# The end of a fused attention and spectral-mix kernel: late rows of Z copied in place, two tiles per store, products begun earlier

## The chip, the cores and the metric

The kernel runs on one core of a Trainium2 chip. The metric is the device time of one execution in microseconds. Three timed runs of the kernel before gave 465.42, 465.90 and 469.37 us, a median of 465.9.

## The reference

A causal attention with a window of 128 positions and a linear bias by head gives x, and a spectral layer mixes x over the sequence:

```python
# q, k, v: (8 batches, 8 heads, 576 positions, 64);  w_r, w_i: (64 modes, 512, 512);  w_ch: (512, 512)
scores = q @ k.T / sqrt(64) - slope[h] * |i - j|     # only 0 <= i - j < 128
x = softmax(scores) @ v                              # as (8, 576, 512)
X = rfft(x, axis=1)[:, :64]                          # Xr + i Xi
Yr = einsum('bmd,mde->bme', Xr, w_r) - einsum('bmd,mde->bme', Xi, w_i)
Yi = einsum('bmd,mde->bme', Xr, w_i) + einsum('bmd,mde->bme', Xi, w_r)
y = irfft(Yr + 1j * Yi, n=576, axis=1)
u = x + y
out = u + relu(u @ w_ch)
```

All inputs and the output are float32. The two sets of mode weights are 134 MB together and are read once.

## The kernel before

The inverse transform is a product with a fixed matrix, FT (128 rows: 64 modes, real and imaginary), so y = FT.T Z, where Z holds a batch's 128 rows of Yr and Yi. Then u @ w_ch = x @ w_ch + FT.T (Z @ w_ch), with Z @ w_ch called ZW. The parts that need only x can be done while the mode weights still come in.

**Stages.** The attention runs over 32 units (8 batches, 4 pairs of heads). The weights of the first head pair's 128 channels are worked off beside it, 3 modes at a time. Then comes the stream: the other 384 channels, one mode per step, for 64 modes. `_load_w` (L578) issues two loads a mode on SP's queue, `wr` and `wi`, into a ring of three buffers. `_modes` does 24 products a mode (L613, L617) into the PSUM tile `acc`, and after each eighth mode and after modes 60, 62 and 64 DVE adds the result to the first pair's part and writes it to `ZT` (L632), which is Z transposed.

The order of each engine's instructions is the order in which the program issues them (a manual schedule). Within the stream, after the products of each mode, the kernel before adds other work:

- **x @ w_ch** for the 36 tiles of 128 positions (`g.seq`: each batch has four tiles; two batches share a ninth with their last 64 positions each). `_xt` transposes the tile (four products into `tp`, a DVE copy to `xT`). `_xw` multiplies it with w_ch into the PSUM tile `xw` (L659, L661), four products of 512 columns, and a fifth that adds x itself where the tile goes by way q. Then `xw` is split into two bf16 parts, `hl`: for each half of the partitions an ACT copy (L666) and a DVE subtraction of that copy (L667). The 36 tiles are spread evenly over the stream.
- **FT** (`_ft`, four times): five transposes and four reorderings, each with four POOL copies into a shared tile `order`, two products and two ACT copies.
- **The early rows of Z and ZW** (`_z_early`, one batch per mode at modes 51 to 58): 16 products of 512 columns into `zwp` and 16 of 128 columns into `zp`, in turn, copied to `ZZ` by ACT and DVE (L688, L689). They give the rows of the modes up to 48 in their final places. The last 16 modes' 32 rows sit in a place that depends on the batch (`_block`).

**PSUM.** In the stream: one bank for `acc`, two buffers each for `tp` and `xw`, one each for `zp` and `zwp`. In the end: three pairs `mm`, `y` (pool `fps`) and two banks for the late rows.

**The end** (`_finish`). After the last mode `_z_late` does the late rows of batches 0 to 3: 16 products for ZW (L700) and 16 for Z (L706) into `late`. Batch 0's are copied to `ZZ` by ACT and DVE (L710, L711); an ACT copy (L713) writes all to `zl`, and three DMAs (L716) carry the other batches' rows to their partitions. The same is done for batches 4 to 7 after tile 4, with four DMAs. Then each tile i goes through:

- `_known`: `hl` into `mm`, and x into `y` (way a only); pairs of products of 512 columns, each for 64 positions (L648). Tiles 0 to 2 have this before the last mode.
- FT.T ZW into `mm`, FT.T Z into `y`, a pair each.
- way a: ACT relu of `mm` to `r` (L766), DVE `y` + `r` (L775). Way q: ACT copies `y` (L769), DVE takes max(`mm`, x) (L770), POOL adds (L778). 19 tiles go by q, 17 by a.
- the store, one DMA of 256 KB a tile (L747), or two of 128 KB for the shared tiles (L749), on SP's queue, from six output buffers.

Of the kernel before, what the change touches and what calls it, by code (L numbers as in the profile page):

```python
# [25 lines left out]
TAIL = 2  # L26

# [6 lines left out]
def kernel(  # L34
# [52 lines left out]
    g.way = ["q" if 2 <= i < len(g.seq) - 3 and i % 5 in (0, 2, 4) else "a" for i in range(len(g.seq))]  # L87

    with tc.manual_schedule(engines={ET.SP, ET.PE, ET.Activation, ET.DVE, ET.Pool}):
        with ExitStack() as wctx:  # L90
# [88 lines left out]
            g.ZZ = zp.tile([P, B, 2, DM], BF16)  # L179
            last = len(GROUPS) - 1  # L180
            for t in line[ahead:]:
                _load_w(g, *t)
            with ExitStack() as xctx:
                xt = xctx.enter_context(tc.tile_pool(name="xts", bufs=2))
                xps = xctx.enter_context(
                    tc.tile_pool(name="xps", bufs=2, space=bass.MemoryType.PSUM))
                eps = xctx.enter_context(
                    tc.tile_pool(name="eps", bufs=1, space=bass.MemoryType.PSUM))
                todo, done, k = list(tiles[last]), 0, 0
                xT = _xt(g, 0, xt, xps)  # L190
                while done < NM - 4:
                    m0, mg = todo.pop(0)
                    _modes(g, last, m0, mg, last=True)
                    done = m0 + mg

                    while k < len(g.seq) and k * (NM - 6) < done * len(g.seq):
                        nxt = _xt(g, k + 1, xt, xps) if k + 1 < len(g.seq) else None
                        _xw(g, k, xT, xps)
                        xT, k = nxt, k + 1
                    if done % 8 == 4 and done < 36:  # L200
                        _ft(g, done // 8, xt, xps)
                    for b in range(B):
                        if m0 <= NM - 14 + b < done:
                            _z_early(g, b, eps)
            g.fps = ctx.enter_context(
                tc.tile_pool(name="fps", bufs=3, space=bass.MemoryType.PSUM))
            g.mm, g.y = {}, {}
            for m0, mg in todo[:-1]:
                _modes(g, last, m0, mg, last=True)
            for i in range(3):  # L210
                _known(g, i)
            _modes(g, last, *todo[-1], last=True)
# [89 lines left out]
def _ft(g, c, pool, psum):  # L302


    nc = g.nc
    S = g.S
    if c == 0:
        cvec = pool.tile([P, 1], FP32, tag="cvec", name="cvec", bufs=1)
        nc.vector.memset(cvec, 2.0 / S)
        nc.vector.memset(cvec[0:1], 1.0 / S)  # L310
        nc.vector.memset(cvec[64:65], 1.0 / S)
        g.FTn = pool.tile([P, S], BF16, tag="FTn", name="FTn", bufs=1)
        for st in range(g.ST):
            n = min(P, S - st * P)
            tp = psum.tile([P, 4, P], BF16, tag="tp", name="tft")[:, 0]
            nc.tensor.transpose(tp[:, 0:n], g.F[0:n, st], g.ident_b[0:n, 0:n])
            nc.vector.tensor_scalar_mul(g.FTn[:, st * P : st * P + n], tp[:, 0:n], cvec)
    order = pool.tile([P, P], BF16, tag="order", name="order", bufs=1)
    src = g.ident_b.rearrange("p (r g m) -> p g r m", r=2, g=4)
    for k in range(4):  # L320
        nc.gpsimd.tensor_copy(  # L321
            order[:, 32 * k : 32 * k + 32].rearrange("p (r m) -> p r m", r=2), src[:, _block(c, k)])
    for a, z in ((0, 512), (512, S)):
        ps = psum.tile([P, g.DM], FP32, tag="xw", name="ftp")
        nc.tensor.matmul(  # L325
            ps[:, 0 : z - a], lhsT=order, rhs=g.FTn[:, a:z], start=True, stop=True)
        nc.scalar.copy(g.FT[:, c, a:z], ps[:, 0 : z - a])
# [324 lines left out]
def _xw(g, n, xT, psum):  # L652
# [4 lines left out]
    xw = psum.tile([P, g.DM], FP32, tag="xw", name="xw")  # L657
# [13 lines left out]
def _z_early(g, b, psum):  # L671


    nc = g.nc
    zp = psum.tile([P, 4, P], FP32, tag="zp", name="zp")
    zwp = psum.tile([P, g.DM], FP32, tag="zwp", name="zwp")
    for et in range(4):
        for k in range(4):
            blk = _block(b % 4, k) % 3
            l = g.ZT[:, et, blk].rearrange("p a m b -> p (a m) b")[:, :, b]  # L680
            ks = slice(32 * k, 32 * k + 32)
            nc.tensor.matmul(
                zwp[ks], lhsT=l, rhs=g.wch[:, et], start=(et == 0), stop=(et == 3),
                tile_position=(0, 32 * k))
            nc.tensor.matmul(
                zp[ks, et], lhsT=l, rhs=g.ident_b, start=True, stop=True,
                tile_position=(0, 32 * k))
    nc.vector.tensor_copy(g.ZZ[:, b, 0], zp.rearrange("p a b -> p (a b)"))  # L688
    nc.scalar.copy(g.ZZ[:, b, 1], zwp)  # L689


def _z_late(g, b0, psum, pool, own):


    nc = g.nc
    late = psum.tile([P, 2, g.DM], FP32, tag="late", name="late")
    for et in range(4):
        for c in range(4):
            l = g.ZT[:, et, 3].rearrange("p a m b -> p (a m) b")[:, :, b0 + c]
            nc.tensor.matmul(  # L700
                late[32 * c : 32 * c + 32, 1], lhsT=l, rhs=g.wch[:, et],
                start=(et == 0), stop=(et == 3), tile_position=(0, 32 * c))
    for et in range(4):
        for c in range(4):
            l = g.ZT[:, et, 3].rearrange("p a m b -> p (a m) b")[:, :, b0 + c]
            nc.tensor.matmul(  # L706
                late[32 * c : 32 * c + 32, 0, et * P : et * P + P], lhsT=l, rhs=g.ident_b,
                start=True, stop=True, tile_position=(0, 32 * c))
    if own:
        nc.scalar.copy(g.ZZ[0:32, b0, 1], late[0:32, 1])  # L710
        nc.vector.tensor_copy(g.ZZ[0:32, b0, 0], late[0:32, 0])  # L711
    zl = pool.tile([P, 2, g.DM], BF16, tag="zl", bufs=1, name="zl")
    nc.scalar.copy(zl, late)  # L713
    for c in range(1 if own else 0, 4):
        ks = slice(32 * c, 32 * c + 32)
        nc.sync.dma_start(out=g.ZZ[ks, b0 + c], in_=zl[ks])  # L716


def _known(g, i):
# [3 lines left out]
    g.mm[i] = g.fps.tile([P, g.DM], FP32, tag="mm", name="mm")  # L723
    g.y[i] = g.fps.tile([P, g.DM], FP32, tag="y", name="y")
    _pair(nc, g.mm[i], [g.ident2] * 2, [g.hl[:, i, h] for h in range(2)], start=True, stop=False)
    if g.way[i] == "a":
        _pair(nc, g.y[i], [g.ident_b[:, 0:64], g.ident_b[:, 64:128]], [x] * 2,
              start=True, stop=False)


def _finish(g):
# [5 lines left out]
    with ExitStack() as fctx:  # L737
        pool = fctx.enter_context(tc.tile_pool(name="fin", bufs=4))
        lps = fctx.enter_context(
            tc.tile_pool(name="lps", bufs=1, space=bass.MemoryType.PSUM, side="right"))  # L740
        _z_late(g, 0, lps, pool, True)
        o, r, y = {}, {}, {}

        def store(i):
            for h, (b, s) in enumerate(g.seq[i][1]):
                if h == 0 and g.seq[i][1][1] == (b, s + 64):
                    nc.sync.dma_start(out=g.out[b, s : s + P, :], in_=o[i])  # L747
                    break
                nc.sync.dma_start(out=g.out[b, s : s + 64, :], in_=o[i][64 * h : 64 * h + 64])  # L749

        for i in range(N + 3):
            if i < N:
                if i >= 3:
                    _known(g, i)
                ft = [g.FT[:, b % 4, s : s + 64] for b, s in g.seq[i][1]]
                _pair(nc, g.mm[i], ft, [g.ZZ[:, b, 1] for b, _ in g.seq[i][1]],
                      start=False, stop=True)
                _pair(nc, g.y[i], ft, [g.ZZ[:, b, 0] for b, _ in g.seq[i][1]],
                      start=(g.way[i] == "q"), stop=True)
            if i == 4:  # L760
                _z_late(g, 4, lps, pool, False)
            j = i - 1
            if 0 <= j < N:
                r[j] = pool.tile([P, g.DM], FP32, tag="r", name="r")
                if g.way[j] == "a":
                    nc.scalar.activation(r[j], g.mm[j], AF.Relu)  # L766
                else:
                    y[j] = pool.tile([P, g.DM], FP32, tag="y", name="ys")
                    nc.scalar.copy(y[j], g.y[j])  # L769
                    nc.vector.tensor_tensor(out=r[j], in0=g.mm[j], in1=g.seq[j][0], op=ALU.max)  # L770
            j = i - 2
            if 0 <= j < N:
                o[j] = pool.tile([P, g.DM], FP32, tag="o", bufs=6, name="o")
                if g.way[j] == "a":
                    nc.vector.tensor_tensor(out=o[j], in0=g.y[j], in1=r[j], op=ALU.add)  # L775
                    store(j)
                else:
                    nc.gpsimd.tensor_tensor(out=o[j], in0=r[j], in1=y[j], op=ALU.add)  # L778
            j = i - 3
# [32 lines left out]
```

## Time and profile before

| | |
|---|---|
| median of three timed runs | 465.9 us |
| the profiled run | 469.43 us, of which its span 467.5 us |
| PE busy | 325.9 us, 70% of the span |
| DVE, ACT, POOL busy | 222.3, 185.7, 150.5 us |
| mean granted clock of TensorE | 0.736 |
| read from memory, written | 163.58 MB, 9.44 MB |
| last DVE addition to ZT begins | 423.62 us |
| first and last issue of a store | 430.8 us, 463.9 us |

The span is the part of the execution that the profile covers; the execution lasts some 2 us longer. In the rows that follow, PEld is TensorE's loading of the stationary operand, which lies beside PE's products, and SPq an issue on SP's queue. The clock is the share of TensorE's full clock that was granted. An arrow in brackets names how long the engine had waited and who ended that wait.

### The profile page before, as it was taken

How to read it: one execution, taken by the hardware profiler on the slowest of the kernel's cores; microseconds unless marked ns; L12 is line 12 of the kernel's file. 1: busy time of each engine (PE TensorE's matmuls, PEld its weight loads, DVE VectorE, ACT ScalarE, POOL GpSimd, SP SyncE). 2: the span in 40 equal slices, each digit the busy share in tenths (PEclk: the TensorE clock that was granted, in tenths of full speed). 3: DMA queues.
4: the chain of work that ended last, by engine and by line, in shares of the span. 5: the costliest groups of instructions: out<-in, count | busy, mean ns of one | idle time of the engine just before them, and what ended most of it. 6: DMA issues, size and time to landing. Idle time of an engine off the chain costs nothing.

```text
span 467.5 us, 13974 instructions
## 1 busy us (share of the span) xinstructions
PE 325.9 (70%) x5914; PEld 226.5 (48%) x5914; DVE 222.3 (48%) x487; ACT 185.7 (40%) x338; POOL 150.5 (32%) x256
## 2 busy tenths in 40 slices
PE   2767798789786896664465666765657699638994
PEld 2655577678574773333243333433334356424552
DVE  8776687577672752242343233332333335202575
ACT  3987677567663730131221212220111223102673
POOL 7896997949961700000000000000000000001594
PEclk9988897887975965567566656755665759955999
DMA  8999999999999989999999999999999999991597
GB/s 251 369 353 324 326 331 391 390 377 388 370 387 400 398 317 381 422 354 406 423 389 425 419 411 425 414 424 422 425 421 424 424 422 413 423 411 55 187 351 276
DMA packets 68718, 174.38 MB, mean 373 GB/s; under 512 B 5712, under 2 KB 22096, under 8 KB 68656
## 3 DMA queue, kind: packets, MB, share of 16 engines
q1 hardware_dynamic: 68272, 172.45, 95.9%
q0 software_dynamic: 384, 1.05, 0.9%
q8 instruction: 46, 0.75, 0.6%
q14 instruction: 16, 0.13, 0.1%
HBM read 163.58 MB, written 9.44 MB: 370 GB/s over the span
## 4 chain that ended last, share of the span: by engine, by line
DMA 57%; PE 27%; issue 4%; DVE 4%; POOL 3%; ACT 3%; SPq 2%; DVEq 0%; ACTq 0%; POOLq 0%
DMA wi<-in_moe_w_i_dram 41%; DMA v<-in_v_dram 7%; PE acc L617 4%; DMA q<-in_q_dram 4%; PE sc L420 4%; PE acc L613 4%; PE av L473 3%; PE xw L661 3%; DMA out_dram<-o 3%; PE tqk L394 2%; PE xt L515 2%; DMA wchf<-in_moe_w_ch_dram 2%; PE tp L639 2%; DMA wr<-in_moe_w_r_dram 1%; POOL qkb L372 1%
## 5 line engine op out<-in xcount | busy, mean ns | idle before, releaser
L666 ACT CAST hl<-xw 64x512 bf16<-64x512 f32 x72 | 41.8, 580 | 161.1 <-PE xw L661 126.9
L617 PEld LDWEIGHTS <-wi 128*128 128x128 bf16 x1024 | 65.4, 105 | 79.1 <-DMA wi<-in_moe_w_i_dram 73.7
L613 PEld LDWEIGHTS <-wr 128*128 128x128 bf16 x1024 | 69.0, 106 | 49.2 <-DMA wr<-in_moe_w_r_dram 28.7
L617 PE MATMUL acc<-Xlast,wi 128*128 128x16 bf16 x768 | 55.3, 193 | 52.3 <-DMA wi<-in_moe_w_i_dram 52.3
L432 ACT ACTIVATE att<-sc 128x512 bf16<-128x512 f32 (+1 forms) x128 | 72.3, 591 | 45.1 <-PE sc L420 44.1
L667 DVE TENSOR_TENSOR hl<-xw,hl 64x512 bf16<-64x512 f32 x72 | 49.6, 689 | 82.1 <-ACT hl L666 81.7
L613 PE MATMUL acc<-Xlast,wr 128*128 128x16 bf16 x768 | 61.7, 193 | 27.1 <-DMA wr<-in_moe_w_r_dram 16.4
L778 POOL TENSOR_TENSOR o<-r,ys 128x512 f32<-128x512 f32 x19 | 23.6, 1275 | 172.8 <-DMA ZZ<-zl 165.6
L383 POOL CAST vb<-v 64x256 bf16<-64x256 f32 x128 | 62.7, 490 | 19.1 <-PE av L473 9.7
L435 DVE TENSOR_TENSOR att<-att,mask 128x512 bf16<-128x512 bf16 x96 | 50.4, 550 | 31.1 <-ACT att L432 30.7
L420 PE MATMUL sc<-qkT,qkT 64*64 64x256 bf16 (+1 forms) x512 | 52.7, 319 | 12.7 <-ACT att L432 5.5
L661 PE MATMUL xw<-wch,xT 128*128 128x512 bf16 x144 | 60.5, 566 | 0.0
L641 DVE COPY xT<-tp 128x512 bf16<-128x512 bf16 x36 | 15.3, 424 | 57.5 <-PE tp L639 57.2
L402 ACT COPY qkT<-tqk 128x576 bf16<-128x576 bf16 x64 | 41.1, 643 | 3.9 <-PE tqk L394 3.9
L420 PEld LDWEIGHTS <-qkT 64*64 64x64 bf16 x512 | 30.0, 124 | 20.5 <-issue 11.1
L394 PE MATMUL tqk<-ident_b,qkb 64*64 64x64 bf16 x1152 | 32.4, 212 | 10.6 <-POOL qkb L372 6.9
L394 PEld LDWEIGHTS <-qkb 64*64 64x64 bf16 x1152 | 31.1, 127 | 13.4 <-POOL qkb L372 8.7
L321 POOL COPY order<-ident_b 128x32 bf16<-128x32 bf16 x16 | 2.6, 210 | 100.0 <-PE ftp L325 83.1
L473 PE MATMUL av<-vb,att 64*128 64x65 bf16 (+1 forms) x1024 | 30.8, 208 | 4.1 <-issue 4.1
L473 PEld LDWEIGHTS <-att 64*128 64x128 bf16 (+1 forms) x1088 | 25.8, 107 | 8.6 <-issue 5.2
L661 PEld LDWEIGHTS <-xT 128*128 128x128 bf16 x144 | 18.8, 136 | 21.8 <-issue 19.3
L372 POOL CAST qkb<-k 128x576 bf16<-128x576 f32 x32 | 27.7, 865 | 0.0
(105 smaller groups left out, 458.4 us busy)
## 6 DMA issues: line engine op xcount, KB each, us to landing
wr<-in_moe_w_r_dram SPq DMA_DIRECT2D x85, 768.0 KB, 8.3
wi<-in_moe_w_i_dram SPq DMA_DIRECT2D x85, 768.0 KB, 9.7
q<-in_q_dram SPq DMA_DIRECT2D x32, 288.0 KB, 7.1
k<-in_k_dram SPq DMA_DIRECT2D x32, 288.0 KB, 7.2
v<-in_v_dram SPq DMA_DIRECT2D x64, 128.0 KB, 6.3
out_dram<-o SPq DMA_DIRECT2D x32, 256.0 KB, 2.7
vt<-in_v_dram POOLq DMA_DIRECT2D x8, 128.0 KB, 6.7
wchf<-in_moe_w_ch_dram SPq DMA_DIRECT2D x2, 512.0 KB, 8.0
```

Of the source, the lines that this page charges most:

```text
L383: g.nc.gpsimd.tensor_copy(o[64 * hh : 64 * hh + 64, i], u.v[64 * i : 64 * i + 64, hh])
L394: g.nc.tensor.transpose(tp[hs, r, :], u.b[w][hs, r], g.ident_b[hs, hs], tile_position=(64 * hh, 64 * hh))
L402: g.nc.scalar.copy(dst.rearrange("c (p r) -> c p r", r=g.R), u.tp[w].rearrange("c r p -> c p r"))
L420: nc.tensor.matmul(sc[hs, r * nq : (r + 1) * nq], lhsT=kT[hs, kt * P + r : kt * P + P : 2], rhs=qT[hs, kt * P : kt * P + nq], start=True, ...
L432: nc.scalar.activation(a[:, :cols], sc[:, :cols], AF.Exp, scale=1.0 / math.sqrt(g.D))
L435: nc.vector.tensor_tensor(out=a, in0=a, in1=g.mask[:, s], op=ALU.mult)
L473: nc.tensor.matmul(av[o, hh, col(t)], lhsT=a[hs, c0 : c0 + m], rhs=vb[hs, 0 : D + 1], start=(j == 0), stop=(j == len(terms) - 1), tile_pos ...
L613: nc.tensor.matmul(o, lhsT=wr[:, a].bitcast(BF16)[:, 1::2][:, c], rhs=X[:, a, 1:3, :, m], start=(a == 0), stop=False)
L617: nc.tensor.matmul(o, lhsT=wi[:, a].bitcast(BF16)[:, 1::2][:, c], rhs=X[:, a, 0:2, :, m], start=False, stop=(a == A - 1))
L661: nc.tensor.matmul(xw, lhsT=xT[:, dt], rhs=g.wch[:, dt], start=(dt == 0 and g.way[n] != "q"), stop=(dt == 3))
L666: nc.scalar.copy(g.hl[own, n, h], xw[own])
L667: nc.vector.tensor_tensor(out=g.hl[other, n, h], in0=xw[own], in1=g.hl[own, n, h], op=ALU.subtract)
```

## The change

1. **x @ w_ch** is done at the modes 28 to 63, one tile at each (`XW`), instead of evenly over all.
2. **FT** is spread: the five transposes at the modes 2 to 6, the four reorderings at 10, 14, 18 and 22, with an `order` tile of four parts that POOL fills at once.
3. **PSUM** is divided anew. `xw`, `zp`, `zwp`, FT's products, and in the end the late rows, take turns in a pool `eps` of two buffers. `tp` has one buffer. The pool `fps` holds two pairs `mm`, `y`; a third comes in the end (`lps`).
4. **The early rows** of Z and ZW come at the modes 54 to 61, all of `zp` first and then all of `zwp`. Batch 0's first 32 rows are then set to zero.
5. **Tiles 0 and 1** are begun in the stream, at the modes 62 and 63: `_known`, and the products of FT with the rows that are there (`_taken`). For these two, the end adds only the 32 late rows.
6. **The late rows** are copied straight from PSUM to their place, batch by batch (`_z_put`, 32 partitions each): ZW by ACT, Z by DVE for the batches 0, 1, 3, 5 and by ACT for the others. There are no DMAs for them. The second half of the late products comes after tile 8.
7. **Ways**: every second tile of a batch goes by q: 16 by q, 20 by a.
8. **Stores**: two neighbouring tiles share an output tile and one DMA of 512 KB, except the first two and the last three tiles and the shared ones. There are six double output tiles.

```diff
+XW = (27, 63)
+EARLY_Z = (54, 55, 56, 57, 58, 59, 60, 61)
+KNOWN = (62, 63)
+FT_ROWS = (2, 3, 4, 5, 6)
+FT_ORDERS = (10, 14, 18, 22)
+LATE_Z = {1: 1, 2: 3, 3: 5, 4: 10, 5: 12, 6: 14, 7: 16}
+LATE_AT = 8
...
-    g.way = ["q" if 2 <= i < len(g.seq) - 3 and i % 5 in (0, 2, 4) else "a" for i in range(len(g.seq))]
+    g.way = ["q" if t[1][0][1] % (2 * P) == P else "a" for t in g.seq]
...
+            g.eps = ctx.enter_context(
+                tc.tile_pool(name="eps", bufs=2, space=bass.MemoryType.PSUM))
+            g.fps = ctx.enter_context(
+                tc.tile_pool(name="fps", bufs=2, space=bass.MemoryType.PSUM))
...
-                    tc.tile_pool(name="xps", bufs=2, space=bass.MemoryType.PSUM))
-                eps = xctx.enter_context(
-                    tc.tile_pool(name="eps", bufs=1, space=bass.MemoryType.PSUM))
+                    tc.tile_pool(name="xps", bufs=1, space=bass.MemoryType.PSUM))
+                k, xT = 0, _xt(g, 0, xt, xps)
+                for m0, mg in tiles[last]:
                     _modes(g, last, m0, mg, last=True)
                     done = m0 + mg
-                    while k < len(g.seq) and k * (NM - 6) < done * len(g.seq):
+                    if done in FT_ROWS:
+                        _ft_rows(g, FT_ROWS.index(done), xt, xps)
+                    if done in FT_ORDERS:
+                        _ft_order(g, FT_ORDERS.index(done), xt)
+                    while k < len(g.seq) and k * (XW[1] - XW[0]) < (done - XW[0]) * len(g.seq):
                         nxt = _xt(g, k + 1, xt, xps) if k + 1 < len(g.seq) else None
-                        _xw(g, k, xT, xps)
+                        _xw(g, k, xT)
                         xT, k = nxt, k + 1
+                    if done in EARLY_Z:
+                        _z_early(g, EARLY_Z.index(done))
+                    if done in KNOWN:
+                        i = KNOWN.index(done)
+                        _known(g, i)
+                        _taken(g, i, last=False)
...
+def _z_early(g, b):
+    nc = g.nc
+    zp = g.eps.tile([P, 4, P], FP32, tag="e", name="zp")
+    zwp = g.eps.tile([P, g.DM], FP32, tag="e", name="zwp")
+    for w, ps in ((0, zp), (1, zwp)):
+        for et in range(4):
+            for k in range(4):
+                blk = _block(b % 4, k) % 3
+                l = g.ZT[:, et, blk].rearrange("p a m b -> p (a m) b")[:, :, b]
+                _z_product(g, ps, w, et, k, l)
+    nc.vector.tensor_copy(g.Z[:, b], zp.rearrange("p a b -> p (a b)"))
+    nc.scalar.copy(g.ZW[:, b], zwp)
...
+def _z_put(g, b):
+    ks = slice(32 * (b % 4), 32 * (b % 4) + 32)
+    if b in (0, 1, 3, 5):
+        g.nc.vector.tensor_copy(g.Z[ks, b], g.late[0][ks])
+    else:
+        g.nc.scalar.copy(g.Z[ks, b], g.late[0][ks])
+    g.nc.scalar.copy(g.ZW[ks, b], g.late[1][ks])
...
+            for b, at in LATE_Z.items():
+                if j == at:
+                    _z_put(g, b)
+            b, s = lo
+            if not whole:
+                for h, (b, s) in enumerate((lo, hi)):
+                    nc.sync.dma_start(out=g.out[b, s : s + 64], in_=oj[64 * h : 64 * h + 64])
+            elif j < 2 or j > N - 4:
+                nc.sync.dma_start(out=g.out[b, s : s + P], in_=oj)
+            elif g.way[j] == "q":
+                nc.sync.dma_start(
+                    out=g.out[b, s - P : s + P].rearrange("(t p) e -> p t e", p=P), in_=o)
```

`_xw` is as before but for its pool: `xw = g.eps.tile([P, g.DM], FP32, tag="e", name="xw")`.

More of the change, by code (lines that the diff above doesn't have):

```diff
@@ L178 @@
             g.hl = zp.tile([P, len(g.seq), 2, DM], BF16)
-            g.ZZ = zp.tile([P, B, 2, DM], BF16)
+            g.Z = zp.tile([P, B, DM], BF16)
+            g.ZW = zp.tile([P, B, DM], BF16)
             last = len(GROUPS) - 1
@@ L182 @@
                 _load_w(g, *t)
+            g.eps = ctx.enter_context(
+                tc.tile_pool(name="eps", bufs=2, space=bass.MemoryType.PSUM))
+            g.fps = ctx.enter_context(
+                tc.tile_pool(name="fps", bufs=2, space=bass.MemoryType.PSUM))
+            g.mm, g.y = {}, {}
             with ExitStack() as xctx:
@@ L185 @@
                 xps = xctx.enter_context(
-                    tc.tile_pool(name="xps", bufs=2, space=bass.MemoryType.PSUM))
-                eps = xctx.enter_context(
-                    tc.tile_pool(name="eps", bufs=1, space=bass.MemoryType.PSUM))
[L189 to L192, printed above, removed]
+                    tc.tile_pool(name="xps", bufs=1, space=bass.MemoryType.PSUM))
+                k, xT = 0, _xt(g, 0, xt, xps)
+                for m0, mg in tiles[last]:
                     _modes(g, last, m0, mg, last=True)
                     done = m0 + mg
-                    while k < len(g.seq) and k * (NM - 6) < done * len(g.seq):
+                    if done in FT_ROWS:
[3 more added lines that the diff above has]
+                    while k < len(g.seq) and k * (XW[1] - XW[0]) < (done - XW[0]) * len(g.seq):
                         nxt = _xt(g, k + 1, xt, xps) if k + 1 < len(g.seq) else None
-                        _xw(g, k, xT, xps)
+                        _xw(g, k, xT)
                         xT, k = nxt, k + 1
[L200 to L212, printed above, removed]
+                    if done in EARLY_Z:
[4 more added lines that the diff above has]
+                        _taken(g, i, last=False)
             mctx.close()
@@ L299, in _block, with _ft_rows @@
     return 3 if k == c else c if k == 3 else k
-def _ft(g, c, pool, psum):
+def _ft_rows(g, st, pool, psum):
     nc = g.nc
     S = g.S
[L307 to L311, printed above, removed]
-        g.FTn = pool.tile([P, S], BF16, tag="FTn", name="FTn", bufs=1)
[L313 to L324, printed above, removed]
+    if st == 0:
+        g.cvec = pool.tile([P, 1], FP32, tag="cvec", name="cvec", bufs=1)
+        nc.vector.memset(g.cvec, 2.0 / S)
+        nc.vector.memset(g.cvec[0:1], 1.0 / S)
+        nc.vector.memset(g.cvec[64:65], 1.0 / S)
+        g.FTn = pool.tile([P, S], BF16, tag="FTn", name="FTn", bufs=1)
+        g.order = pool.tile([P, 4, P], BF16, tag="order", name="order", bufs=1)
+        src = g.ident_b.rearrange("p (r g m) -> p g r m", r=2, g=4)
+        for c in range(4):
+            for k in range(4):
+                nc.gpsimd.tensor_copy(
+                    g.order[:, c, 32 * k : 32 * k + 32].rearrange("p (r m) -> p r m", r=2),
+                    src[:, _block(c, k)])
+    n = min(P, S - st * P)
+    tp = psum.tile([P, 4, P], BF16, tag="tp", name="tft")[:, 0]
+    nc.tensor.transpose(tp[:, 0:n], g.F[0:n, st], g.ident_b[0:n, 0:n])
+    nc.vector.tensor_scalar_mul(g.FTn[:, st * P : st * P + n], tp[:, 0:n], g.cvec)
@@ L325, in _ft, with _ft_order @@
+def _ft_order(g, c, pool):
+    nc = g.nc
+    for a, z in ((0, 512), (512, g.S)):
+        ps = g.eps.tile([P, g.DM], FP32, tag="e", name="ftp")
         nc.tensor.matmul(
-            ps[:, 0 : z - a], lhsT=order, rhs=g.FTn[:, a:z], start=True, stop=True)
+            ps[:, 0 : z - a], lhsT=g.order[:, c], rhs=g.FTn[:, a:z], start=True, stop=True)
         nc.scalar.copy(g.FT[:, c, a:z], ps[:, 0 : z - a])
@@ L649, in _pair, with _xw @@
             out[64 * h : 64 * h + 64], lhsT=lhsT[h], rhs=rhs[h], tile_position=(0, 64 * h), **kw)
-def _xw(g, n, xT, psum):
+def _xw(g, n, xT):
     nc = g.nc
     x = g.seq[n][0]
-    xw = psum.tile([P, g.DM], FP32, tag="xw", name="xw")
+    xw = g.eps.tile([P, g.DM], FP32, tag="e", name="xw")
     if g.way[n] == "q":
@@ L668, in _xw @@
             out=g.hl[other, n, h], in0=xw[own], in1=g.hl[own, n, h], op=ALU.subtract)
-def _z_early(g, b, psum):
+def _z_early(g, b):
     nc = g.nc
[L675 to L689, printed above, removed]
@@ L692, in _z_late @@
[L692 to L716, printed above, removed]
+    zp = g.eps.tile([P, 4, P], FP32, tag="e", name="zp")
@@ new lines, in _z_early @@
+    zwp = g.eps.tile([P, g.DM], FP32, tag="e", name="zwp")
+    for w, ps in ((0, zp), (1, zwp)):
+        for et in range(4):
+            for k in range(4):
+                blk = _block(b % 4, k) % 3
[3 more added lines that the diff above has]
+    nc.scalar.copy(g.ZW[:, b], zwp)
+    if b == 0:
+        nc.vector.memset(g.Z[0:32, b], 0.0)
+        nc.gpsimd.memset(g.ZW[0:32, b], 0.0)
@@ new lines, in _z_product, with _z_late @@
+def _z_product(g, ps, w, et, k, l):
+    ks = slice(32 * k, 32 * k + 32)
+    if w:
+        g.nc.tensor.matmul(
+            ps[ks], lhsT=l, rhs=g.wch[:, et], start=(et == 0), stop=(et == 3),
+            tile_position=(0, 32 * k))
+    else:
+        g.nc.tensor.matmul(
+            ps[ks, et], lhsT=l, rhs=g.ident_b, start=True, stop=True,
+            tile_position=(0, 32 * k))
+def _z_late(g, b0):
+    zp = g.eps.tile([P, 4, P], FP32, tag="e", name="zlp")
+    zwp = g.eps.tile([P, g.DM], FP32, tag="e", name="zlw")
+    for w, ps in ((0, zp), (1, zwp)):
+        for et in range(4):
+            for c in range(4):
+                l = g.ZT[:, et, 3].rearrange("p a m b -> p (a m) b")[:, :, b0 + c]
+                _z_product(g, ps, w, et, c, l)
+    g.late = (zp.rearrange("p a b -> p (a b)"), zwp)
@@ new lines, in _z_put, with _taken @@
+def _z_put(g, b):
+    ks = slice(32 * (b % 4), 32 * (b % 4) + 32)
+    if b in (0, 1, 3, 5):
+        g.nc.vector.tensor_copy(g.Z[ks, b], g.late[0][ks])
+    else:
+        g.nc.scalar.copy(g.Z[ks, b], g.late[0][ks])
+    g.nc.scalar.copy(g.ZW[ks, b], g.late[1][ks])
+def _taken(g, i, rows=slice(0, P), last=True):
+    nc = g.nc
+    for w, out, z in ((1, g.mm[i], g.ZW), (0, g.y[i], g.Z)):
+        for h, (b, s) in enumerate(g.seq[i][1]):
+            nc.tensor.matmul(
+                out[64 * h : 64 * h + 64], lhsT=g.FT[rows, b % 4, s : s + 64],
+                rhs=z[rows, b],
+                start=(w == 0 and g.way[i] == "q" and rows.stop == P), stop=last,
+                tile_position=(0, 64 * h))
@@ L722, in _known @@
     x = g.seq[i][0]
-    g.mm[i] = g.fps.tile([P, g.DM], FP32, tag="mm", name="mm")
-    g.y[i] = g.fps.tile([P, g.DM], FP32, tag="y", name="y")
+    pool = g.lps if i % 3 == 2 else g.fps
+    g.mm[i] = pool.tile([P, g.DM], FP32, tag="mm", name="mm")
     _pair(nc, g.mm[i], [g.ident2] * 2, [g.hl[:, i, h] for h in range(2)], start=True, stop=False)
+    g.y[i] = pool.tile([P, g.DM], FP32, tag="y", name="y")
     if g.way[i] == "a":
@@ L738, in _finish @@
         pool = fctx.enter_context(tc.tile_pool(name="fin", bufs=4))
-        lps = fctx.enter_context(
+        g.lps = fctx.enter_context(
             tc.tile_pool(name="lps", bufs=1, space=bass.MemoryType.PSUM, side="right"))
[L741 to L749, printed above, removed]
@@ L751, in _finish @@
-        for i in range(N + 3):
+        _z_late(g, 0)
+        _z_put(g, 0)
+        for i in range(N + 1):
             if i < N:
-                if i >= 3:
+                if i < len(KNOWN):
+                    _taken(g, i, slice(0, 32))
+                else:
                     _known(g, i)
[L755 to L761, printed above, removed]
-            j = i - 1
[L763 to L779, printed above, removed]
-            if 0 <= j < N and g.way[j] == "q":
-                store(j)
@@ new lines, in _finish @@
+                    _taken(g, i)
+            if i == LATE_AT:
+                _z_late(g, 4)
+            j = i - 1
+            if j < 0:
+                continue
+            x, (lo, hi) = g.seq[j]
+            whole = hi == (lo[0], lo[1] + 64)
+            if not (whole and g.way[j] == "q"):
+                o = pool.tile([P, 2, g.DM], FP32, tag="o", bufs=6, name="o")
+            oj = o[:, 1 if g.way[j] == "q" else 0]
+            if g.way[j] == "a":
+                r = pool.tile([P, g.DM], FP32, tag="r", name="r")
+                nc.scalar.activation(r, g.mm[j], AF.Relu)
+                nc.vector.tensor_tensor(out=oj, in0=g.y[j], in1=r, op=ALU.add)
+            else:
+                ys = pool.tile([P, g.DM], FP32, tag="y", name="ys")
+                nc.scalar.copy(ys, g.y[j])
+                r = pool.tile([P, g.DM], FP32, tag="r", name="r")
+                nc.vector.tensor_tensor(out=r, in0=g.mm[j], in1=x, op=ALU.max)
+                nc.gpsimd.tensor_tensor(out=oj, in0=r, in1=ys, op=ALU.add)
```

## The prediction

> **What bounds the kernel now.** I read the page's slices first, then the chain of waits from 390 us on, then the stages of the end, then the timeline around one x @ w_ch step.
>
> ```profile
> PE   2767798789786896664465666765657699638994
> PEclk9988897887975965567566656755665759955999
> GB/s 251 369 353 324 326 331 391 390 377 388 370 387 400 398 317 381 422 354 406 423 389 425 419 411 425 414 424 422 425 421 424 424 422 413 423 411 55 187 351 276
> ```
>
> The DMA engines move about 420 GB/s up to slice 36 and PE has room there. Then reading stops, slice 37 moves 55 GB/s, and the end follows. The chain shows the same:
>
> ```profile
> 411.73 0.20 PE acc L617
> ...
> 422.74 0.20 PE acc L617
> ...
> 423.62 0.30 DVE ZT L632
> ```
>
> Three weight buffers: the products of one mode free the buffer of the mode three later, so 11.0 us pass between modes 60 and 63 (counted from 0), 3.7 us a mode. PE may take 3.7 us a mode and cost nothing. The last mode starts at 422.74; the last sum of Z is ready at 423.92. What lies behind takes 467.50 - 423.92 = 43.6 us, in four stages (columns: stage, length, busy time of PE, PEld, DVE, ACT, POOL, granted clock, DMA share, GB/s):
>
> ```profile
> 423.92:427.05 3.13, 2.36 (x34) 1.22 (x34) 0.02 (x1) 0.57 (x1) 0.00 (x0) 0.50 0.00 0
> 427.05:435.61 8.56, 7.59 (x66) 3.97 (x65) 3.26 (x6) 4.16 (x7) 1.26 (x1) 0.70 0.25 84
> 435.61:460.80 25.19, 23.81 (x206) 13.99 (x207) 18.52 (x29) 17.63 (x31) 21.51 (x18) 1.00 0.82 287
> 460.80:467.50 6.70, 0.59 (x6) 0.11 (x2) 2.07 (x3) 0.81 (x2) 0.87 (x1) 0.91 0.80 297
> ```
>
> The first two are late products at half clock and the trip of Z's late rows through DMA; the third is bound by PE (23.8 of 25.2 us busy), not by stores.
>
> **Modes 1 to 53: nothing.** FT's five transposes, eight products and sixteen order copies stay as many and go into modes 2 to 22, from which x @ w_ch has left; POOL, which makes the copies (16 x 0.21 us), has nothing else there. From mode 28 on each mode carries one x @ w_ch step. At half clock that is 0.85 for the mode (422.74 to 423.59), 0.38 for four transposes (379.04 to 379.42) and 2.04 for four or five products of 0.45 (five: 379.42 to 381.68), 3.27 us in all, under 3.7. The stream hides it, with 0.4 us to spare; each 0.1 us beyond that would cost 2.6 us over the 26 modes. xw's way out of its buffer (2.8 us, below) also ends inside the mode, and the single transpose buffer is free a mode earlier.
>
> **Modes 54 to 61 (indices 53 to 60): a new wait, eight times.** Now xw, zp and zwp take turns in two buffers of the pool eps. Each step is xw, zp, zwp: zp gets the other buffer, and zwp gets the one that this step's xw has just filled. PE can't begin zwp's products until xw has been copied out, and the next mode's products, whose end frees the buffer for SP's next weight load, queue behind it. Before, zp and zwp had buffers of their own. (The two fills of batch 0's first rows, on DVE and POOL, fall into this wait.) How long copying out takes:
>
> ```profile
> 398.51 0.45 PE L682 MATMUL zwp<-wch,ZT 128*32 128x512 bf16 x4
> 398.62 0.58 ACT L666 CAST hl<-xw 64x512 bf16<-64x512 f32 x1 [1.56 <-PE xw L661]
> ...
> 399.23 0.68 DVE L667 TENSOR_TENSOR hl<-xw,hl 64x512 bf16<-64x512 f32 x1 [2.04 <-ACT hl L666]
> ...
> 399.95 0.58 ACT L666 CAST hl<-xw 64x512 bf16<-64x512 f32 x1 [0.75 <-DVE hl L667]
> ...
> 400.56 0.69 DVE L667 TENSOR_TENSOR hl<-xw,hl 64x512 bf16<-64x512 f32 x1 [0.65 <-ACT hl L666]
> ```
>
> ACT, DVE, ACT, DVE strictly in turn: 398.51 (PE done with xw) to 401.25, with 0.05 for the signal 2.79 us. Only zp (0.34 at full clock) fits inside. The second copy waits for the first subtraction; the groups list it 36 times out of 36 (28.4 us). So one step is:
> - full clock: mode 0.75 (386.46 to 387.21), transposes 0.22, xw 0.96 or 1.17 (mean 1.06; 387.43 to 388.39), wait 2.79, zwp 0.92 (the late products, 432.61 to 433.53): 5.74 us
> - half clock: 0.85 + 0.38 + 2.04 + 2.79 + 1.72 (423.96 to 425.68): 7.78 us
>
> Both exceed 3.7, so from index 53, which starts at 422.74 - 10 x 3.705 = 385.7, PE sets the pace and the ring waits for PE. Which clock is granted?
>
> ```profile
> 371.40:374.80 3.40, 1.74 (x27) 0.98 (x23) 2.42 (x4) 1.39 (x3) 0.00 (x0) 0.90 1.03 428
> 374.80:378.20 3.40, 3.18 (x56) 1.82 (x54) 0.95 (x2) 0.65 (x2) 0.00 (x0) 0.50 1.00 412
> ...
> 398.40:401.80 3.40, 2.79 (x58) 1.93 (x58) 1.89 (x3) 1.75 (x3) 0.00 (x0) 1.00 1.00 411
> ```
>
> A stretch with PE busy for 1.74 of 3.40 us lost the full clock, though its longest gap was 1.66 us; one with 2.79 kept it. A full-clock step would be busy for about 3.3 of 5.74 us (57%) and lose it; a half-clock step has 5.4 us of work without a gap, and behind such a burst (PE busy without a gap from 378.5 to 385.9) the clock rose to 1.00. So it will swing, and I take the middle of the two, 6.76 us a step: 54.1 us.
>
> The Trainium skill, page "TensorE: Matmul & The Clock Gate", section "What's actually happening", has the gate close only after an idle window of about 3.4 us. By that rule the 2.8 us gaps would leave the clock full and the time would be that of the first rival below. The rows above speak against it.
>
> **The last three modes.** Behind index 61 stand transposes, xw 34 (five products) and tile 0's known and early products (four pairs of 0.215 at full clock, of 0.43 at half); behind index 62 xw 35, tile 1's three pairs, and the last mode. The last ZT addition stands on DVE behind xw 35's subtractions, 2.73 us after that xw, which is later than the products themselves (0.65 + 0.75). Full clock: (0.75 + 0.22 + 1.17 + 0.86) + (0.75 + 0.96) + 2.73 = 7.4; half: 10.6. PE works without gaps here, so I take the middle, 9.0. With 0.3 for the addition Z is complete at 385.7 + 54.1 + 9.0 + 0.3 = 449.1 instead of 423.9: 25.2 us later (15.5 at full clock throughout, 34.9 at half).
>
> **The end.** Gone: seven DMAs for Z's late rows with their 1.01 us copies, the half clock at its start (PE arrives busy), and 14 of the 40 store issues. Added: twelve 32-row copies on ACT (0.57 each) and four on DVE (0.68), beside PE's work. From Z complete: late products 0.34 + 0.92 at full clock, ACT's copy 0.57, signals 0.1: 1.9 us. Then PE: the late four rows of tiles 0 and 1, four pairs, 0.9; of the other 34 tiles 19 by way a (four pairs, 0.86) and 15 by way q (three, 0.645), 26.0; the second late products 1.3: 28.1 us without a wait. The third stage above got 206 matmuls x 0.1075 = 22.1 us done in 25.2, 88%, part of its waits being for output buffers (DVE 4.4 us), of which there are now twice as many. At 88% 28.1 becomes 31.9; I take 30, between. After PE's last: relu 0.6, addition 0.7, two issues 1.1, landing 2.4, closing 0.7, signals: 5.6 to 6.7 (stage four); 5.9 taken. Sum 37.8 instead of 43.6: 5.8 us saved, 3.1 to 8.0 by the bounds. Stores don't bind: 9.4 MB at the 408 GB/s of 460 to 463 us is 23 us.
>
> Sum: 467.5 + 25.2 - 5.8 = 486.9 of span; the profiled run took 469.4 for its 467.5, so 488.8, and the median of 465.9 lies 3.5 below it: 485.3.
>
> **Rivals.**
> 1. The clock stays full through the eight steps (windows as at 384.8 to 408 us): +15.5 - 5.8, 475.6 us. Against it: 57% busy. 0.17.
> 2. It stays at half: +34.9 - 5.8, 495.0 us. For it: 0.5 or 0.6 in most slices of the stream; against it: the bursts of 5.4 us. 0.11.
> 3. The wait is absorbed and the kernel is faster: if ACT's second copy starts with the first and PE waits less, the ring covers it. Break-even is where Z is complete 5.8 us late, a step of 4.5 us at full clock, a wait of 1.6 instead of 2.8. With steps of 3.7, only the shorter end counts: 460.1. Against it: 36 waits out of 36. 0.06, and 0.04 for ending near break-even.
>
> **The numbers.** My forecast has 0.62 and 485 us. The range runs from 472 (rival 1 with the best end: 465.9 + 15.5 - 8.0 = 473.4) to 497 (rival 2 with the weakest: 497.7). About 1% is what a measurement of this kernel tells from no change. Faster 0.06, within 1% 0.04, slower 0.90.
>
> **What would show it.** Right: eight waits of PE at zwp's weight loads for DVE's hl, some 2.4 us each; SP issuing weights 5.7 to 7.8 us apart behind mode 54 and a lower GB/s there; the last ZT addition near 449 us; full clock in the first us of the end, no ZZ DMA, and some 38 us behind the addition. Wrong: weight issues still 3.7 us apart after mode 54, the addition before 430 us, or an end longer than 41 us.

## The result, and the profile after

The changed kernel takes 492.97 us (median of four runs, 491.96 to 497.64), the kernel before 467.63 in the runs beside it: a ratio of 1.056, 95% interval 1.047 to 1.065. It is slower, inside the range, 7.7 us above the forecast.

The page's slices, those of before being 11.7 us and these 12.3 us long:

```profile
PE   2776987889779852333233267676776776678994
PEclk9979797887957955555555567767678667777898
GB/s 255 377 331 331 331 342 374 381 399 375 394 380 401 370 395 423 426 423 423 426 424 424 425 423 423 423 425 410 407 421 421 366 199 254 229 157 23 171 278 301
```

From slice 16 to slice 31 the stream runs at some 420 GB/s (404 to 426), as it did before. Then five slices move 157 to 366 GB/s: the weights come only as fast as PE takes them, and SP issues them 6.8 to 7.6 us apart. The waits of PE between 385 and 455 us (who waited for whom, us in total, times, longest):

```profile
PE zwp L705 <- DVE hl L678: 17.7, 8, 2.3
PE zlp L709 <- DVE ZT L643: 1.5, 1, 1.5
PE mm L742 <- ACT ZW L734: 0.7, 1, 0.7
```

Eight waits of zwp for the subtractions of hl, as forecast; none for weights. One step in the timeline of PE, ACT and DVE:

```profile
389.49 1.91 PE L672 MATMUL xw<-wch,xT 128*128 128x512 bf16 x4
...
391.33 0.66 PE L709 MATMUL zp<-ident_b,ZT 128*32 128x128 bf16 x16
391.44 0.58 ACT L677 CAST hl<-xw 64x512 bf16<-64x512 f32 x1 [2.38 <-PE xw L672]
392.05 0.69 DVE L678 TENSOR_TENSOR hl<-xw,hl 64x512 bf16<-64x512 f32 x1 [1.89 <-ACT hl L677]
392.77 0.58 ACT L677 CAST hl<-xw 64x512 bf16<-64x512 f32 x1 [0.75 <-DVE hl L678]
393.38 0.69 DVE L678 TENSOR_TENSOR hl<-xw,hl 64x512 bf16<-64x512 f32 x1 [0.65 <-ACT hl L677]
...
394.13 1.93 PE L705 MATMUL zwp<-wch,ZT 128*32 128x512 bf16 x16 [2.14 <-DVE hl L678]
```

From zp's start at 391.33, right behind xw's last product, to zwp's at 394.13 there are 2.80 us, the forecast wait of 2.79. The products of index 53 (the 54th mode) start at 381.05 us and those of index 61 at 439.28: 58.2 us for eight steps, 7.3 us each on average (6.8 to 7.6). The last addition to ZT is over at 447.5 us. What follows, in four stages (columns: stage, length, busy time of PE, PEld, DVE, ACT, POOL, granted clock, DMA share, GB/s):

```profile
447.50:458.00 10.50, 9.71 (x68) 4.12 (x70) 4.00 (x7) 5.15 (x9) 2.52 (x2) 0.51 0.13 50
458.00:471.00 13.00, 12.58 (x132) 6.65 (x130) 9.71 (x15) 10.59 (x21) 6.37 (x5) 1.00 0.60 223
471.00:485.40 14.40, 13.45 (x121) 8.41 (x119) 11.74 (x19) 11.16 (x20) 10.43 (x9) 1.00 0.85 317
485.40:491.30 5.90, 0.00 (x0) 0.00 (x0) 0.54 (x1) 0.00 (x0) 1.02 (x1) 0.77 0.68 252
```

The end takes 491.3 - 447.5 = 43.8 us; before it took 43.6. So in these two traces Z is complete 23.6 us later, and the new end, which was to save 5.8, saved nothing: its first 10.5 us run at half clock.

The 23.6 us hold a lead that has nothing to do with the eight waits. SP's load of `wr` for index 51, issued ahead of the first early rows, shows it, first in the kernel before and then in the changed one:

```profile
368.13 0.33 SPq L578 DMA_DIRECT2D wr<-in_moe_w_r_dram  x1
```

```profile
363.47 0.33 SPq L589 DMA_DIRECT2D wr<-in_moe_w_r_dram  x1
```

The changed kernel's stream is 4.7 us ahead there. From this load until Z is complete the kernel before takes 55.8 us and the changed one 84.0: the late modes lost 28.2 us.

### The profile page after: what moved, and what is told of

Read it like the earlier page. It is cut to its first block, busy times and chain, and to the rows that moved or that the text cites. A ratio compares the mean times of both kernels' runs of the same rounds, so it can differ in the third digit from the quotient of the medians.

```text
span 491.3 us, 13940 instructions
## 1 busy us (share of the span) xinstructions
PE 321.9 (66%) x5925; PEld 223.4 (45%) x5925; DVE 224.8 (46%) x491; ACT 188.7 (38%) x347; POOL 146.9 (30%) x254
## 4 chain that ended last, share of the span: by engine, by line
DMA 48%; PE 33%; ACT 6%; issue 5%; DVE 5%; SPq 1%; POOL 1%; POOLq 0%; ACTq 0%; DVEq 0%
DMA wi<-in_moe_w_i_dram 39%; DMA v<-in_v_dram 5%; PE sc L431 5%; PE acc L628 4%; PE acc L624 4%; PE xw L672 3%; DVE hl L678 3%; PE xt L526 3%; PE zwp L705 3%; PE av L484 2%; PE tqk L405 2%; DMA q<-in_q_dram 2%; ACT hl L677 2%; DMA wr<-in_moe_w_r_dram 2%; PE mm L742 2%
## 5 line engine op out<-in xcount | busy, mean ns | idle before, releaser
L624 PE MATMUL acc<-Xlast,wr 128*128 128x16 bf16 x768 | 62.9, 194 | 30.1 <-DMA wr<-in_moe_w_r_dram 28.8
L394 POOL CAST vb<-v 64x256 bf16<-64x256 f32 x128 | 66.3, 518 | 22.5 <-PE av L484 13.0
L672 PE MATMUL xw<-wch,xT 128*128 128x512 bf16 x144 | 54.0, 514 | 0.0
L800 POOL TENSOR_TENSOR o<-r,ys 128x512 f32<-128x512 f32 x16 | 20.3, 1272 | 76.4 <-DVE r L799 73.0
L405 PE MATMUL tqk<-ident_b,qkb 64*64 64x64 bf16 x1152 | 32.5, 213 | 11.7 <-POOL qkb L383 6.0
L643 DVE TENSOR_TENSOR ZT<-acc,ZTa 128x512 bf16<-128x512 f32 (+2 forms) x10 | 5.8, 585 | 71.1 <-PE acc L628 71.0
L338 ACT CAST FT<-ftp 128x512 bf16<-128x512 f32 (+1 forms) x8 | 2.8, 402 | 82.5 <-PE ftp L336 82.5
```

The lines of the kernel that those rows point to most:

```text
L394: g.nc.gpsimd.tensor_copy(o[64 * hh : 64 * hh + 64, i], u.v[64 * i : 64 * i + 64, hh])
L405: g.nc.tensor.transpose(tp[hs, r, :], u.b[w][hs, r], g.ident_b[hs, hs], tile_position=(64 * hh, 64 * hh))
L624: nc.tensor.matmul(o, lhsT=wr[:, a].bitcast(BF16)[:, 1::2][:, c], rhs=X[:, a, 1:3, :, m], start=(a == 0), stop=False)
L672: nc.tensor.matmul(xw, lhsT=xT[:, dt], rhs=g.wch[:, dt], start=(dt == 0 and g.way[n] != "q"), stop=(dt == 3))
```

## The experiments

In what follows "Z complete" is the end of the last addition to ZT, and "the end" is the span less that, both from the run's trace. Times are medians, ratios those to the kernel before on the same chip with their 95% intervals. "From index 51" is the time from SP's load of `wr` for index 51, as above, to Z complete: it leaves out how early the stream stood there, which differs from run to run.

**Is it the shared buffer, or the amount of work?** The banks of mm and y lie idle until mode 62; zp and zwp get them. Nothing else changes: the same work in the same modes.

```diff
-    zp = g.eps.tile([P, 4, P], FP32, tag="e", name="zp")
-    zwp = g.eps.tile([P, g.DM], FP32, tag="e", name="zwp")
+    zp = g.fps.tile([P, 4, P], FP32, tag="mm", name="zp")
+    zwp = g.fps.tile([P, g.DM], FP32, tag="y", name="zwp")
```

> The changed kernel, but zp and zwp take the PSUM banks of mm and y, which are free until mode 62, instead of the two buffers shared with xw. Theory A (the shared buffer: zwp waits until this step's xw is copied out): the eight waits (17.7 us by the trace of the changed kernel) are gone, a step is 3.3 us at full clock, Z is complete 20 to 24 us sooner, near 424 to 428 us, and the time is 468 to 474 us. Rival B (the work itself, xw and the early rows in the same modes, does not fit into 3.7 us at half clock, 5.4 us a step): Z is complete near 436 to 440 us and the time is 481 to 486 us.

466.06 us, ratio 0.996 (0.992 to 0.999); Z complete at 421.9 us, the end 43.0. From index 51 it is 56.1 us, as in the kernel before (55.8). The time and Z complete lie some 2 us below what theory A named; the stream stood 2.3 us earlier at index 51 (365.82 us) than in the kernel before. PE's waits between 385 and 460 us begin with

```profile
PE acc L628 <- DMA wi<-in_moe_w_i_dram: 3.5, 8, 1.1
PE mm L742 <- ACT ZW L734: 0.7, 1, 0.7
```

PE waits for weights again; no wait for hl is left, and SP issues weights some 3.7 us apart. zwp's products take 0.38 to 0.39 us in all eight steps, the value of full clock, where the changed kernel had a median of 0.62. So the wait also cost the clock, and without it PE keeps the full clock and the work fits. That is theory A; the amount of work alone (rival B, 481 to 486 us) is out.

**The same from the other side.** The changed kernel with all x @ w_ch ten modes sooner, so that no xw precedes the early rows:

```diff
-XW = (27, 63)
+XW = (17, 53)
```

> The changed kernel with x @ w_ch at the modes 18 to 53 instead of 28 to 63, so that no xw is left in the modes of the early rows; the two shared buffers stay. Theory A: zwp waits no more, Z is complete near 424 us, the end takes 44 us at half clock, the time is 466 to 472 us. If sharing the buffers costs even without xw (zp and zwp waiting for each other's copies), Z is complete later than 430 us and the time is above 474 us.

465.40 us, ratio 0.996 (0.992 to 1.000), Z complete at 420.4 us, from index 51 55.8 us, the end 43.6. The two buffers may be shared by zp and zwp alone at no cost. zwp's products took 0.63 us in all eight steps here, the value of half clock: with xw gone the step is short enough for that. The time is just below the forecast 466, and Z was complete sooner than the 424 named.

**Half of the dose.** Batches 0 to 3 in the shared buffers, 4 to 7 in the banks of mm and y:

```diff
+    own = b >= 4
+    zp = (g.fps if own else g.eps).tile([P, 4, P], FP32, tag="mm" if own else "e", name="zp")
+    zwp = (g.fps if own else g.eps).tile([P, g.DM], FP32, tag="y" if own else "e", name="zwp")
```

> The changed kernel, with the early rows of the batches 4 to 7 in the banks of mm and y and those of the batches 0 to 3 still in the buffers shared with xw. Theory A (each shared step costs its wait and the clock lost by it, 7.2 us instead of 3.7): four steps of 3.5 us remain and the four others gain back some 0.4 us each; Z is complete near 434 to 436 us and the time is 477 to 481 us. If the delay came from a single event or a threshold, it would be near 466 or near 493 us.

480.65 us (two runs), ratio 1.027 (1.018 to 1.035), Z complete at 434.4 us. From index 51 it takes 69.9 us, where the run with no shared step takes 56.1 and the changed kernel 84.0: four steps cost 13.8 us, eight cost 27.9. The loss goes by the step.

**The shared buffer alone, in the kernel before.** There zp and zwp are put into the two buffers of xw, and nothing else is changed:

```diff
-    zp = psum.tile([P, 4, P], FP32, tag="zp", name="zp")
-    zwp = psum.tile([P, g.DM], FP32, tag="zwp", name="zwp")
+    zp = psum.tile([P, 4, P], FP32, tag="xw", name="zp")
+    zwp = psum.tile([P, g.DM], FP32, tag="xw", name="zwp")
...
-                            _z_early(g, b, eps)
+                            _z_early(g, b, xps)
```

> The kernel before, with one thing changed: zp and zwp take the two buffers of xw instead of banks of their own. Its x @ w_ch is spread over the whole stream, so four of the eight steps of early rows have an xw just ahead. Theory A (the shared buffer alone makes the loss): such a step takes 6.2 us at full and 8.4 us at half clock, the steps between them 2.3 to 3.2 us, so a pair of steps costs 1 to 4 us more than the 7.4 us that the stream gives it: 4 to 14 us in all, 471 to 481 us. Rival (the loss needs the other parts of the change): 465 to 469 us.

472.79 us, ratio 1.011 (1.007 to 1.016), Z complete at 427.3 us (before: 423.9), from index 51 62.0 us (before: 55.8). Its PE waits:

```profile
PE zp L683 <- DVE hl L665: 9.2, 4, 2.4
```

Four waits of 2.3 us cost 6.2 us from index 51, inside the forecast 4 to 14; that the steps between them, with no xw, give the other 3 us back fits, but wasn't measured by itself. In Z complete only 3.4 us show, because the stream stood 2.8 us earlier at index 51. The other parts of the change aren't needed for the loss; with an xw in each of these modes it becomes large.

**Why did the end save nothing?** PE's clock around the last addition in the changed kernel (stage, length, PE busy, granted clock, DMA share, GB/s):

```profile
441.06:444.47 3.41, 3.41 (x42) 1.00 0.02 5
444.47:447.88 3.41, 1.95 (x43) 0.96 0.00 0
447.88:451.29 3.41, 2.68 (x36) 0.50 0.00 0
```

PE had the full clock, then waited 1.5 us for the addition behind xw 35's subtractions, and had half of it until 458 us. The test fills that gap:

```diff
+            fill = g.eps.tile([P, g.DM], FP32, tag="e", name="fill")
+            for _ in range(7):
+                nc.tensor.matmul(fill, lhsT=g.ident_b, rhs=g.wch[:, 0], start=True, stop=True)
```

> The changed kernel with seven more products of 512 columns (their result is not used) between the last mode and the late products, so that PE is not idle for the 1.5 us in which it waits for the last addition to ZT. Theory D (the end saves nothing because the clock falls to half in that gap): the late products take 1.3 instead of 2.4 us and the first tiles run at full clock, the end is 39 us instead of 43.8, the time 487 to 489 us. Rival E (the end is bound by ACT's copies and DVE, whatever the clock): end 43 to 44 us, time 492 to 494 us.

489.86 us, ratio 1.047 (1.042 to 1.053). Z complete at 448.9 us, 1.4 us later than in the changed kernel's trace; the end 40.3 instead of 43.8. Its first 4 us now read

```profile
448.95:452.95 4.00, 3.27 (x51) 1.76 (x51) 1.43 (x4) 1.93 (x4) 0.00 (x0) 1.00 0.00 0
```

By the medians, products that nobody uses made the kernel 3.1 us faster. The two ratios' intervals overlap (1.047 to 1.065 without the filler), so the trace has to carry the point: full clock, and an end 3.5 us shorter. Theory D holds in kind; the end is 1.3 us longer than its 39, and the time 0.9 above its range.

**The last xw one mode sooner**, with zp and zwp in banks of their own:

```diff
-XW = (27, 63)
+XW = (26, 62)
```

> As the run before it (zp and zwp in banks of their own), and x @ w_ch at the modes 27 to 62 instead of 28 to 63, so that the last addition to ZT no longer stands behind the subtractions of the last xw. Theory A: Z is complete about 1 us sooner than in the run before it; PE has less to do in the last two modes, so the late products run at half clock and the end stays near 44 us: 466 to 473 us. Rival C (the end is long because the addition is late and the clock falls in that gap): the end shrinks to some 39 us, 461 to 467 us.

468.47 us, ratio 1.001 (0.997 to 1.005), Z complete at 423.7 us, the end 43.6. PE waits 0.4 us for the last addition, no less than in the run with the banks alone, and the clock fell already ahead of that, behind a stretch with little work for PE (stage, length, PE busy, granted clock, DMA share, GB/s):

```profile
418.56:421.98 3.42, 1.82 (x30) 0.98 0.59 248
```

The granted clock was 0.50 from 422.0 to 432 us, and the end isn't shorter, near the 44 us of theory A: an earlier addition alone doesn't cure it, as rival C had it. Z was complete 1.8 us later than in the run it is compared with, not 1 us sooner, because the stream stood 2.0 us later at index 51 (367.86 us, there 365.82); from there it took 55.9 us, there 56.1. This holds in general: among the eight kernels whose stream is bound by the weights Z was complete between 418.3 and 423.9 us, but from index 51 all take 55.8 to 57.5 us. Most of what varies lies ahead of the modes where these kernels differ in the early rows; what makes it vary there isn't known.

**Both remedies, and what else binds the end.** First the banks of their own together with the filler (six products before the last mode, two behind it):

```diff
+                    if done == NM - 1:
+                        fill = g.eps.tile([P, g.DM], FP32, tag="e", name="fill")
+                        for _ in range(6):
+                            nc.tensor.matmul(fill, lhsT=g.ident_b, rhs=g.wch[:, 0], start=True, stop=True)
+            for _ in range(2):
+                nc.tensor.matmul(fill, lhsT=g.ident_b, rhs=g.wch[:, 0], start=True, stop=True)
```

> The run with zp and zwp in banks of their own (Z complete at 421.95 us, end 42.95 us, TensorE at half clock from 422.3 to 429.3 us), and eight more products of 512 columns whose result is not used: six before the last mode, two between it and the late products. Theory D (the end saves little because the clock falls in PE's gaps around the last mode): full clock through the end, end about 40.3 us as with the filler in the changed kernel, span about 462.5, time 462 to 465 us. Rival E (ACT and DVE bind the end, the clock does not matter): end 42 to 43 us, time 465 to 467 us.

463.59 us, ratio 0.988 (0.983 to 0.993); Z complete at 422.0 us, the end 40.2. The first stages of the end with the banks alone, and then with banks and filler (columns as in the four stages above):

```profile
421.95:425.95 4.00, 3.27 (x38) 1.60 (x40) 0.68 (x1) 1.12 (x2) 0.00 (x0) 0.56 0.00 0
425.95:429.95 4.00, 4.00 (x24) 1.56 (x22) 3.19 (x5) 2.12 (x5) 1.26 (x1) 0.58 0.22 85
```

```profile
422.00:426.00 4.00, 3.27 (x51) 1.77 (x52) 1.45 (x3) 1.95 (x4) 0.00 (x0) 1.00 0.00 0
426.00:430.00 4.00, 3.81 (x36) 2.03 (x33) 3.28 (x6) 3.90 (x8) 2.54 (x2) 1.00 0.34 131
...
438.00:442.00 4.00, 3.81 (x32) 2.15 (x33) 3.19 (x5) 3.93 (x8) 2.64 (x3) 1.00 0.68 262
```

At full clock 51 products fit where there were 38. And ACT is now full (3.90 and 3.93 of 4.00 us) where it copies the late rows. So next all Z rows go to DVE:

```diff
-    if b in (0, 1, 3, 5):
+    if True:
         g.nc.vector.tensor_copy(g.Z[ks, b], g.late[0][ks])
```

> As the run before it, and all of Z's late rows copied by DVE (ACT copies ZW alone: 8 copies instead of 12). Theory F (where the late rows of the batches 4 to 7 are copied, ACT binds: busy for 3.9 of 4 us): 1 to 2 us less than the run before it. Rival: DVE takes ACT's place, the same within 0.5 us.

460.34 us, ratio 0.984 (0.979 to 0.988), the best of all. But of the 4.3 us in span only 0.6 are in the end (39.6 instead of 40.2), where alone the edit acts; Z was complete at 418.3 us in that profile, and 2.4 us of this lead were there at index 51 (362.11 us instead of 364.51). DVE is nearly full in its turn, and ACT still is:

```profile
421.90:425.90 4.00, 3.81 (x36) 2.08 (x34) 3.87 (x7) 3.88 (x8) 2.14 (x2) 1.00 0.34 130
```

The end lies at the rival's edge: half a microsecond shorter, not 1 to 2. Then stores by single tiles, with Z's copies shared between ACT and DVE as in the change:

```diff
-            elif j < 2 or j > N - 4:
-                nc.sync.dma_start(out=g.out[b, s : s + P], in_=oj)
-            elif g.way[j] == "q":
-                nc.sync.dma_start(
-                    out=g.out[b, s - P : s + P].rearrange("(t p) e -> p t e", p=P), in_=o)
+            else:
+                nc.sync.dma_start(out=g.out[b, s : s + P], in_=oj)
```

> As the first run of these (own banks, filler), and every tile stored by itself, 256 KB a store. Theory G (a pair holds the first tile's store back until the second is there, and the last stores come late): 0.5 to 1.5 us shorter. Rival H (stores are off the path of the end, PE and ACT set it): the same within 0.5 us. If pairing saves time in SP's issues, up to 2 us longer.

462.54 us, ratio 0.988 (0.983 to 0.993), the end 39.7: no difference that the times can tell, 0.5 us by the trace. Theory G and rival H meet at this half microsecond, so neither is settled; pairing the stores costs no more than that here. Both edits at once:

> The run with banks of their own, filler and Z's late rows copied by DVE, with every tile stored by itself. The two last steps shortened the end by about 0.5 us each, by the traces; if they add up, the end is 39 us, the time 457 to 462 us, 0.980 to 0.985 of the kernel before. If the stores then bind, the same as with pairs.

462.20 us, ratio 0.989 (0.983 to 0.996), the end 39.5, Z complete at 421.9. In the end they don't add up (39.6 and 39.7 became 39.5), and this run's time fits that the 460.3 above owes most of its lead to where the stream ended.

## Why the prediction was right, point by point

- **The wait.** Right in place, number and size: eight, 2.80 us from zp to zwp in seven of them, and 2.42 in the first, where zp itself had waited 0.4. The runs with banks of their own, with xw moved away, with half of the banks and with the shared buffers in the kernel before settle that it is the cause.
- **The clock in the steps.** It stayed at half from 386.2 to 399.8 us, two of the steps, and from there on it swung, as forecast:

```profile
406.96:410.37 3.41, 1.39 (x28) 0.96 0.84 296
410.37:413.78 3.41, 3.41 (x43) 0.54 0.57 184
413.78:417.19 3.41, 1.08 (x24) 0.96 0.71 294
417.19:420.60 3.41, 3.41 (x48) 0.54 0.38 102
```

  A stretch at full clock holds the wait and is followed by one at half clock, full of work; behind that the clock is full again for the next wait. The full clock thus falls on the waiting. A step took 7.3 us, not the 6.76 of the middle between 5.74 and 7.78: the middle was 0.5 us too low, 4.1 us over eight steps. Both rivals on the clock (full throughout, half throughout) are out. The Trainium skill, page "TensorE: Matmul & The Clock Gate", section "What's actually happening", lets the gate close after an idle window of some 3.4 us; here it closed after stretches with gaps of at most 2.3 us. Its length of a window fits the 3.41 us in which the rows above alternate: the clock changed at 406.7, 410.1, 413.5, 416.9 and 420.3 us.
- **Z complete.** Forecast 449.1, measured 447.5, and that it came so near is luck. Index 53 started at 381.05, not 385.7: the stream was ahead by 4.7 us, which hid that the eight steps were 4.1 us longer than forecast. The last three modes with the addition took 8.2 us, forecast 9.3; the addition did stand behind xw 35's subtractions. Most of the lead isn't shown to come from the change: 1.8 us were there at the first load of the stream (173.36 us, before 175.12), ahead of all that was changed, and from that load to index 51's the kernel before took 193.0 us, the changed one 190.1, and the run with the shared buffers in the kernel before, whose stream runs the same instructions as before up to there, 190.3.
- **The end.** Here a step failed: "the half clock at its start (PE arrives busy)" was listed as gone. PE did arrive at full clock, but the gap before the addition, which follows from the same text's numbers (2.73 - 0.65 - 0.75 = 1.3 us; measured 1.5), was not carried into the clock. 43.8 us instead of 37.8, beyond the 41 that the prediction had named as a sign of being wrong. With the gap filled it was 40.3, so 3.5 of the 6.0 us go with the clock. The rest is spread over the sum: in the run with the filler its three terms, forecast as 1.9, 30 and 5.9 us, measure 2.1 (Z complete at 448.95 to the first tile's product at 451.08), 31.6 (to PE's last product, over at 482.66) and 6.5, each of the last two inside its bounds. Moving Z's copies to DVE and single stores took half a microsecond each by the traces. The shortest end, 39.5 us, is still 1.7 above the forecast; that rest wasn't tried further.
- **Down to the median.** The 3.5 us between the profiled run and the median of before were taken off; the changed kernel's profiled run (493.11 us) lay on its median. With -1.6 for Z, +6.0 for the end and +3.4 here the 485.3 become 493.1. This 3.4 and the lead of 4.7 us may be one thing seen twice: in the profiled run of before the stream stood later than in all the others, and that run was 3.5 us above its median.
- **The rival on the other side**, a wait absorbed by the ring, needed one of 1.6 us or less. It stayed at 2.8, and is out.

## What to carry to other kernels

When tiles of one kind are put into the buffers of another, write out whose turn it is: a buffer that was just filled and leaves over two engines by turns stalls the first engine for the whole of that way (2.8 us here). Look for banks that lie idle in that stage before sharing busy ones; here the same work in the banks of the next stage cost nothing. And when a stage is planned for a warm TensorE, count the gaps just ahead of it too, since 1.5 us of waiting, by the run that filled it, cost the end 3.5 us. Last, compare two traces from a common point just ahead of the change: here the streams of two kernels that are the same up to there stood 5.0 us apart before the modes in question began (362.11 and 367.13 us at index 51).

## What the runs showed of the hardware

Filling gaps with products that nobody uses shortened the end in both kernels where it was tried: seven of 512 columns took it from 43.8 to 40.3 us in the changed kernel, and eight from 43.0 to 40.2 in the one with banks of its own (medians 492.97 and 489.86 us, 466.06 and 463.59).

The granted clock changed only at times that lie a multiple of about 3.41 us apart: in the changed kernel every 3.41 us between 399.8 and 440.8 us, in the kernel before at 374.1, 384.3 and 408.2 us. Cut along these times, PE's busy time in a stretch at full clock told whether the next one had it (kernel before; stage, length, PE busy, granted clock, DMA share, GB/s):

```profile
370.66:374.07 3.41, 2.14 (x34) 0.99 1.03 429
374.07:377.48 3.41, 2.82 (x51) 0.51 1.00 412
401.38:404.79 3.41, 2.31 (x50) 1.00 1.00 416
404.79:408.20 3.41, 0.83 (x23) 1.00 1.03 428
```

Behind 2.14 us the full clock was lost, behind 2.31 it was kept. In the changed kernel it was lost behind the 1.96 us of 444.18 to 447.60, with the one gap of 1.5 us. Where between 2.14 and 2.31 us the border lies, and whether it is the same elsewhere, these traces don't show.
